# A transformer block on one NeuronCore: the first MLP sweep in steps of two tiles, output weights by quarter rows, two token tiles loaded by ScalarE's queue, and a new instruction order

## The chip, the cores and the metric

The kernel runs on one core of a Trainium2 chip. The core has five engines with a queue of instructions each: TensorE (PE in the profile; PEld is its loading of weights), VectorE (DVE), ScalarE (ACT), GpSimd (POOL) and SyncE (SP), which here only issues DMAs. ScalarE can issue DMAs as well. Each engine works its queue in order and waits on semaphores where it needs another engine's result. The metric is the device time of one execution in microseconds (us).

## The reference

The input is one sequence `x` of 2048 tokens and 512 channels, in bfloat16. A conditioning vector `c` gives six rows of 512 numbers by which two sub-blocks are shifted, scaled and gated.

```python
sa, ca, ga, sb, cb, gb = split((silu(c) @ w_mod), 6)
h = layernorm(x) * (1 + ca) + sa
x = x + ga * A(h)                       # attention
h = layernorm(x) * (1 + cb) + sb
out = x + gb * B(h)                     # MLP that mixes tokens
# A: 32 heads of 16 channels; a token sees itself and 7 others, 2, 4, ... 14 tokens back
q, k, v = split(h @ wqkv)
attn = softmax(q . k[t - 2w] / 4, w = 0..7);  A = (sum_w attn * v[t - 2w]) @ wo
# B: layernorm again, then over the TOKEN axis
u = gelu(layernorm(h).T @ w1 + b1)      # 2048 -> 1792
B = (u @ w2 + b2).T                     # 1792 -> 2048
```

## The kernel before

The 2048 tokens are 16 tiles of 128. They go through the attention half in five chunks of 2, 4, 4, 4 and 2 tiles (`SIZES`). For each chunk: LayerNorm statistics of a tile on VectorE or ScalarE (`ln1s`, `ln1v`, then `rstd1_`, `nb1_` for a group) and the normalized tile (`n1_`, on any of three engines); a transpose (`tr` on TensorE and its evictions `hT` in chunks 0 and 1, by DMA, `xt`, later); the projections `qkv<chunk>_<q, k or v><part>` on TensorE and their evictions `ev`; the products q*k on VectorE (`qk<chunk>_<0..3>`, 2.28 us each in a chunk of four tiles), summed over the head's channels by TensorE (`red`); the softmax, a chain over four engines: `max` (VectorE), `sub` (TensorE), `exp` (ScalarE), `esum` (TensorE), `rcp` (ScalarE), `smB` (VectorE). The probabilities and the values are then spread over the partitions by DMAs (`a2_<chunk>_<0..3>` and `vd<chunk>_<0..3>`), multiplied on VectorE (`pv`, again 2.28 us each), summed by TensorE (`pvacc`), evicted (`oev`) and multiplied with the output weights (`wo`). `x1_`, `ln2..`, `n2_`, `aff` and `ln3..`, `h3_` make the two further normalizations. For chunk 0 and 1 the unscaled projection weights are used, and the scale `a1col` is applied by the evictions `hT`; the scaled weights (`wsc`) serve the later chunks. `a1col` comes from `c`: `ld_c`, a small matmul `cps`, `silu_exp` (ScalarE), `silu_dve` (VectorE), and `modcols1` on TensorE, which also needs `ld_wmod1`.

The MLP needs every token for every output, so its first matrix product is cut into sweeps. `MIX` has two groups of rows of `u`: tiles 0 to 6 run over token tiles 0-5, 6-10 and 11-15, tiles 7 to 13 over token tiles 0-9 and 10-15. A sweep's partial sum is parked (`park`, ScalarE, in the tile `gT`), added later (`padd`) and put through `gelu`. In the order text, `mlp1_<sweep>_<row tile>_<first token tile>` is one step of such a sweep; its matmuls read `h3` of its token tiles. A step is issued as a whole on TensorE; before, the first sweep's steps hold four token tiles:

```python
steps = list(range(s_lo, s_hi, 4)) if not last else sorted(
```

`mlp2_<tile>` is the second product, `fin` and `st_out` finish and store a tile.

Nothing is ordered by a scheduler at run time. Each piece of work is named, and the text `ORDER` lists all of them in the order in which they are issued; each engine's queue is this list with the other engines' entries left out. A letter behind the name chooses the engine (`:a` ScalarE, `:d` VectorE, `:p` GpSimd, `:s` SyncE), `:q` cuts a matmul into four that write 32 partitions each, `:n` leaves an added identity matmul out, and `fill:62` issues matmuls of the identity that nobody reads, 62 times 128 columns in pieces of 512 and the rest of 128. `_Graph.schedule` (line 86) turns the text into the list and assigns the buffers; `ln_stats` (379), `build_chunk` (609) and the loops from line 918 on define the pieces. All instructions are recorded in one helper, so that every row of the profile has line 142 and pieces are told by their tiles: `psS` and `psL` are PSUM, `xx` the tokens, `big` the products, `vD` and `a2sb` what the two kinds of DMA write, `wst` staged weights, `woq` the output weights, `junk` the output of statistics on ScalarE.

`woq` holds 128 partitions of 4 x 512. Its source rows are numbered 16 h + 4 q + l; partition 32 l + h, column block q. Before, four DMAs (`ld_wo0` to `ld_wo3`) each bring one `l`: 32 partitions, four rows of 1 KB in each.

Of the kernel before, what the change touches and what calls it, by code (L numbers as in the profile page):

```python
# [196 lines left out]
ln1s11:a ln1s10:d ln1v10 ld_x_3_12 wsc1_1:p qvb0 qvb_cp0:d ev0_00:a qkv1_13 ld_wrow1 ld_b2 ln1s13:d qkv1_03 ev0_02:a  # L197
ln1v11 qkv1_10:q ln1v13 n1_9:a ev1_03:a qk0_1 qk0_0 ld_b1 ev1_13:a ld_wo3 ld_wqkv2 ld_x_4_14 ev1_10:a qkv1_00 ev1_00:a
wsc0_2:p qvb1 qvb_cp1:a red0_0 red0_1 qkv0_22:q ld_wo2 ld_wmod2 ln1s12:a qkv0_20 qk0_2 qk0_3 qk1_0 red0_2 red0_3
ev0_22:a ev0_20:a wsc0_1:a mask ln1v12 rstd1_3 qkv1_01 max0 ld_wrow3 ev1_01:a ld_wrow0 qk1_3 ld_wrow2 qkv1_11 sub0  # L200
# [6 lines left out]
oev0_0:a oev0_2:a smB1 wsc2_0:a wo0:q st_row1 ev2_12:a qk2_2 ev2_13:a qk2_3 wsc2_2:a x1_0:a wo1 x1_1:a vd1_2 qkv3_03
qkv2_22 biascols_cp:a a2_1_0:a qkv2_23 rstd1_4 a2_1_3:s nb1_4 qkv2_20 qkv2_21:q a2_1_2:s a2_1_1:s vd1_0 ln2q1:a
ln2q0:a n1_14:a ln2m0 ev3_03:a rstd2_0 red2_1 pv1_3 red2_2 n1_15:a red2_3 ev2_20:a vd1_1 nb2_0 ev2_22:a qkv3_11
ev2_21:a pvacc1_3 qkv3_12:q max2 sub2 n2_0:a ld_row1 qkv3_01 ev2_23:a qkv3_00:q ev3_11:a ev3_12:a oev1_3:a pv1_0  # L210
halo_k3:a exp2 pvacc1_0 oev1_0:a qkv3_02:q halo_v2:a qkv3_10:q ev3_02:a esum2 ev3_00:a vd2_3 xt14 pv1_2 rcp2 pvacc1_2
oev1_2:a pv1_1 pvacc1_1 oev1_1:a ev3_10:a n2_1:p aff0 ev3_01:a ln3s0:a smB2 qk3_0 qkv3_13:q vd2_1 qk3_2 wo5:q x1_5:a
wo2:q wo4 x1_2:a ev3_13:a x1_4:a qk3_1 wo3 a2_2_2:s ld_w1_0_512 ln2q5:a ln2q4:a ln2m4 x1_3:a vd2_2 red3_0 ln3s1:a
qkv3_22 ln2q2:a ln2q3:a ln3v0 qkv3_20:q rstd2_4 a2_2_3:s qkv3_21 ev3_20:a qkv4_00 ev3_21:a a2_2_1:s qk3_3 ln2m2
rstd2_2 qkv4_02 ev4_02:a a2_2_0:s pv2_3 nb2_2 n2_2:p qkv3_23 red3_1 vd2_0 ev4_00:a ld_w1_0_0 nb2_4 n2_4:a ld_w2_1
ev3_23:a red3_2 halo_v3:p ev3_22:a halo_v4:a vd3_0 red3_3 qkv4_20:q qkv4_12 max3 sub3 pv2_1 exp3 vd3_1 pvacc2_3 esum3
# [5 lines left out]
oev3_1:a park0_0:a park0_1:a ln2q6:a red4_0 pv3_3 pvacc3_3 oev3_3:a ln2q8:a pv3_2 park0_2:a mlp1_0_6_0:q pvacc3_0
ld_w1_0_896 pvacc3_2 mlp1_0_6_4:q oev3_2:a qk4_1 red4_1 vd4_0 ln2m6 rstd2_6 mlp1_0_4_0:q qk4_3 nb2_6 mlp1_0_4_4:q
oev3_0:a qk4_2 n2_8:d wo12:q n2_6:a n2_9:a ld_w2_2 park0_3:a park0_4:a park0_5:a x1_12:a park0_6:a ln2q12:a
mlp1_0_7_0:q mlp1_0_8_0:q ld_w2_4 n2_7:d aff6 ln3s7:a red4_2 red4_3 wo11:q x1_11:a ld_w2_0 max4 ld_w1_0_1152
mlp1_0_9_0 ln3s6:d ln3s8:d ln3s9:d sub4 ln3v6 ln3v9 exp4 wo13:n ln3v7 mlp1_0_10_0 ld_w1_0_1408 ln3v8 rstd3_6 x1_13:d
vd4_1 vd4_2 wo10:n nb3_6 h3_6:p h3_7:a mlp1_0_12_0 ln2q13:a mlp1_0_12_4 esum4 rcp4 x1_10:d mlp1_0_9_4 ln2m12 smB4
h3_8:d h3_9:p rstd2_12 nb2_12 n2_13:d a2_4_2:a mlp1_0_7_4 mlp1_0_7_8 mlp1_0_8_4 a2_4_0:a ln2q11:a n2_12:d aff12
mlp1_0_8_8 ln2q10:a a2_4_3:s mlp1_0_10_4 mlp1_0_9_8 mlp1_0_10_8 ln2m10 rstd2_10 inj1_3:qn park0_7:a park0_8:a a2_4_1:s
park0_9:a park0_10:a pv4_1 nb2_10 n2_11:a mlp1_0_11_0 mlp1_0_11_4 mlp1_0_11_8 pv4_0 pvacc4_0 pvacc4_1 n2_10:a  # L230
mlp1_0_12_8:q pv4_3 pv4_2 pvacc4_2 aff10 ln3s11:d park0_11:a pvacc4_3 ld_w1_0_1664 mlp1_0_13_0:q inj1_6:n oev4_0:a
oev4_2:a wo14:q ln3s10:a ln3s13:d x1_14 ln2s14 ld_w1_1_0 mlp1_0_13_4 park0_12:a ln2v14 wo15 ln3s12:a ld_w2_3 rstd2_14
ln3v11 x1_15 mlp1_0_13_8 ln3v10 rstd3_10 ln3v13 park0_13:a nb2_14 inj1_1:qn inj1_2:qn ln3v12 rstd3_12 n2_14:p ln2s15
ln2v15 nb3_10 mlp1_1_2_6 inj1_0:qn mlp1_1_0_6 mlp1_1_1_6 inj1_5:n ld_w1_1_640 aff14 mlp1_1_5_6 rstd2_15 nb2_15 n2_15:p
ln3s14:d ln3v14 h3_10:a mlp1_1_2_10 mlp1_1_1_10 aff15 rstd3_14 nb3_12 h3_12:p mlp1_1_0_10 park1_0:+ nb3_14 ln3s15:d
ln3v15 mlp1_1_5_10 mlp1_1_3_6 inj1_4:qn park1_1:+ rstd3_15 nb3_15 h3_15:d mlp1_1_4_6 mlp1_1_6_6 mlp1_1_6_10
ld_w1_1_896 ld_w1_2_0 h3_13:p mlp1_1_3_10 h3_14:a mlp1_1_4_10 ld_w1_1_1408 park1_2:+ park1_3:+ park1_4:+ h3_11:p
mlp1_1_7_10 padd1_7 gelu7 mlp1_1_8_10 padd1_8 mlp1_1_9_10 padd1_9 gelu9 mlp1_1_10_10 ld_w1_2_640 park1_5:+ mlp1_2_2_11
mlp1_2_3_11 mlp1_2_3_14 park1_6:+ padd2_3 mlp1_2_0_11 gelu3 gelu8 mlp1_2_2_14 padd2_2 mlp1_2_0_14 padd2_0 gelu0
ld_w2_5 mlp1_2_4_11 mlp1_2_4_14 padd2_4 padd1_10 mlp1_2_1_11 mlp1_2_1_14 gelu4 padd2_1 mlp1_2_6_11 ld_w2_7 gelu2  # L240
mlp1_2_5_11 mlp1_2_5_14 gelu1 padd2_5 gelu5 mlp1_1_11_10 mlp1_1_13_10 padd1_11 padd2_6 gelu6 mlp1_1_12_10 padd1_12
padd1_13 ld_w2_15 gelu11 gelu10 gelu12 mlp2_0_0 mlp2_0_0b gelu13 mlp2_0_0c fin0_0 st_out0_0 mlp2_4_0 mlp2_8_0 fin4_0
st_out4_0 fin8_0 mlp2_1_0 fin1_0 st_out1_0 st_out8_0 mlp2_6_0 ld_w2_13 mlp2_5_0 mlp2_3_0 mlp2_2_0 fin2_0 fin3_0 fin5_0
mlp2_7_0 ld_w2_9 ld_w2_11 mlp2_9_0 mlp2_10_0 st_out2_0 st_out3_0 fin6_0 st_out6_0 fin10_0 gsc fpre st_out5_0
st_out10_0 mlp2_14_0 fin9_0 st_out9_0 fin7_0 st_out7_0 fin14_0 mlp2_11_0 fin11_0 st_out11_0 st_out14_0 mlp2_12_0
fin12_0 mlp2_13_0 st_out12_0 fin13_0 st_out13_0 mlp2_15_0 fin15_0 st_out15_0 mlp2_15_1 fin15_1 st_out15_1 mlp2_15_2
# [822 lines left out]
```

## Time and profile before

| | |
|---|---|
| median of three runs | 203.14 us (202.55 to 203.84) |
| the profiled execution's own time | 202.81 us |
| its span, first to last instruction | 200.9 us |
| granted TensorE clock | 1.00 |
| instructions | 4468 |
| moved by DMA | 35.94 MB, mean 179 GB/s |

The costliest groups (line, engine, operation, out<-in, shapes, count, then busy us, mean ns of one, and the idle time just before them with what ended most of it):

```profile
L142 PE MATMUL psS<-h,wst 128*128 128x512 bf16 (+1 forms) x308 | 51.1, 379 | 0.1
L142 DVE TENSOR_TENSOR big<-a2sb,vD 128x4096 bf16<-128x4096 bf16 (+1 forms) x20 | 36.5, 1856 | 2.0 <-DMA vD<-v_sb 1.3
L142 DVE TENSOR_TENSOR big<-q_sb,k_f 128x4096 bf16<-128x4096 bf16 (+1 forms) x20 | 36.5, 1857 | 0.2 <-ACT q_sb L142 0.2
L142 ACT ACTIVATE junk<-xx 128x512 bf16<-128x512 bf16 x26 | 16.4, 632 | 3.0 <-DMA xx<-in_A_x_dram 1.4
```

Matmuls are pipelined: a 512-column one is listed with 379 ns, but the next can start 216 ns after it. So a busy TensorE may still be waiting, and its work is better counted by starts. Idle time is listed before the instruction that ends it.

### The profile page before, as it was taken

To read this page: it belongs to the slowest core of one execution; us is meant where nothing else is said; L and a number is where in the kernel's file an instruction comes from. 1 tells how busy PE (TensorE), PEld (TensorE's weight loads), DVE (VectorE), ACT (ScalarE), POOL (GpSimd) and SP (SyncE) were. 2 spreads that over 40 slices of the span, in tenths; PEclk is the share of its full clock that TensorE was granted. 3 is DMA by queue.
4 is the path that set the end of the run, shared out by engine and by line. 5 is a ranking of instruction groups with operands and counts; after the bars stand their busy time and mean duration, and the time that the engine had idled before them with its cause. 6 is when DMAs were issued, how large, how long until landed. Compare 5 with 4: busy or idle time off the path is not lost.

```text
span 200.9 us, 4468 instructions
## 1 busy us (share of the span) xinstructions
PE 190.1 (95%) x1778; PEld 95.1 (47%) x1778; DVE 159.1 (79%) x240; ACT 128.2 (64%) x308; POOL 18.1 (9%) x45
## 2 busy tenths in 40 slices
...
GB/s 169 330 378 286 304 198 89 208 217 86 259 3 280 291 303 123 172 302 284 237 151 135 31 167 220 157 129 298 337 41 26 26 77 328 211 93 26 52 82 52
DMA packets 53936, 35.94 MB, mean 179 GB/s; under 512 B 24476, under 2 KB 50716, under 8 KB 53916
## 3 DMA queue, kind: packets, MB, share of 16 engines
...
q14 instruction: 6, 0.05, 0.1%
...
## 4 chain that ended last, share of the span: by engine, by line
PE 66%; ACT 19%; DVE 9%; issue 3%; DMA 1%; SPq 0%; ACTq 0%; DVEq 0%
PE psS L142 64%; ACT junk L142 6%; DVE big L142 5%; ACT v_sb L142 3%; PE psL L142 2%; ACT h L142 2%; DVE h L142 2%; ACT xx L142 1%; ACT o_sb L142 1%; ACT q_sb L142 1%; ACT k_f L142 1%; DMA xx<-in_A_x_dram 1%; ACT hT L142 1%; ACT lv L142 1%; DVE woq L142 1%
## 5 line engine op out<-in xcount | busy, mean ns | idle before, releaser
L142 PEld LDWEIGHTS <-wst 128*128 128x128 bf16 (+1 forms) x482 | 34.9, 101 | 34.8 <-issue 4.5
L142 PE MATMUL psS<-h,wst 128*128 128x512 bf16 (+1 forms) x308 | 51.1, 379 | 0.1
L142 DVE TENSOR_TENSOR big<-a2sb,vD 128x4096 bf16<-128x4096 bf16 (+1 forms) x20 | 36.5, 1856 | 2.0 <-DMA vD<-v_sb 1.3
L142 DVE TENSOR_TENSOR big<-q_sb,k_f 128x4096 bf16<-128x4096 bf16 (+1 forms) x20 | 36.5, 1857 | 0.2 <-ACT q_sb L142 0.2
L142 DVE SCALAR_TENSOR_TENSOR h<-psS,bcol,rows_bc 128x512 f32<-128x512 f32 (+2 forms) x17 | 12.1, 709 | 22.6 <-PE psS L142 22.4
L142 PE MATMUL psS<-hT,w_qkv 128*32 128x512 bf16 (+3 forms) x300 | 29.3, 347 | 0.0
L142 PEld LDWEIGHTS <-w_qkv 128*32 128x32 bf16 (+1 forms) x342 | 19.7, 109 | 16.6 <-issue 3.3
L142 PE MATMUL psS<-gT,big 128*128 128x512 bf16 x112 | 24.8, 379 | 0.0
L142 ACT ACTIVATE junk<-xx 128x512 bf16<-128x512 bf16 x26 | 16.4, 632 | 3.0 <-DMA xx<-in_A_x_dram 1.4
L142 PEld LDWEIGHTS <-big 128*128 128x128 bf16 x144 | 12.0, 97 | 13.2
L142 PE MATMUL psS<-woq,o_sb 128*32 128x512 bf16 (+1 forms) x148 | 16.6, 380 | 0.7 <-ACT o_sb L142 0.7
L142 ACT ACTIVATE gT<-psS,bcol 128x512 bf16<-128x512 f32 x14 | 9.0, 685 | 8.6 <-DVE psS L142 8.4
L142 ACT ACTIVATE h<-xx,nb,rs 128x512 bf16<-128x512 bf16 x16 | 12.7, 812 | 2.4 <-DVE nb L142 2.4
L142 DVE TENSOR_TENSOR psS<-psS,gT 128x512 f32<-128x512 f32 x14 | 9.3, 694 | 6.1 <-PE psS L142 6.1
L142 POOL TENSOR_SCALAR h<-xx,rs,nb 128x512 bf16<-128x512 bf16 x9 | 6.9, 766 | 75.2 <-DVE mv L142 33.1
L142 PE MATMUL psS<-hT,wst 128*128 128x256 bf16 (+2 forms) x88 | 11.7, 343 | 0.8 <-ACT hT L142 0.8
L142 PEld LDWEIGHTS <-group 128*32 128x32 bf16 x288 | 6.5, 95 | 11.0 <-DVE big L142 4.0
L142 DVE TENSOR_TENSOR h<-h,xx 128x512 bf16<-128x512 f32 (+2 forms) x17 | 11.1, 652 | 0.7
L142 PE MATMUL psS<-big,group 128*32 128x512 bf16 (+1 forms) x160 | 9.6, 339 | 2.1 <-DVE big L142 2.0
L142 DVE TENSOR_TENSOR h<-h,rows_bc 128x1024 bf16<-128x1024 bf16 (+2 forms) x16 | 11.0, 690 | 0.4
L142 ACT ACTIVATE q_sb<-psS,qvb 128x512 bf16<-128x512 f32 (+1 forms) x20 | 11.2, 609 | 0.0
L142 ACT ACTIVATE v_sb<-psS,qvb 128x512 bf16<-128x512 f32 (+1 forms) x20 | 10.9, 603 | 0.0
...
## 6 DMA issues: line engine op xcount, KB each, us to landing
...
```

What stands on the lines that cost most here:

```text
L142: r = fn(*a, **k)
```

## The change

Four edits and a new list:

- The steps of the first sweep start at token tiles 0, 2, 4, 6 and 10 instead of every fourth tile from the sweep's first. The steps of the middle sweep (6, 10) stay.
- The output weights are brought by `q`: each of the four DMAs now writes all 128 partitions, one row of 1 KB in each.
- The loads of the first chunk's tiles and of chunk 1's two pairs may be issued by ScalarE. In the list one of them is: `ld_x_1_2`, ahead of `ld_c` and of the load of ScalarE's table.
- The choice of queues for `a2_` is written as a shared constant, which changes nothing.
- `ORDER` is another list. Some 40 pieces change their engine, 25 matmul steps become quartered and 21 whole ones, and there are eight fills (4, 64, 4, 13, 1, 1, 18, 14) instead of two (62, 17).

```diff
-ident act_table halo0 ld_x0 ln1s0:d ln1v0 ld_x1 ld_x_1_4 ld_c cps ln1s1:a ln1v1 rstd1_0 ln1s4:d consts nb1_0 ld_x_1_2
-ld_wmod1 fill:62 ln1s5:a ln1v4 ln1s3:d ln1s2:d ld_x_2_8 ld_wqkv1 ln1v3 silu_exp n1_0:a n1_1:p ld_x_2_6 ln1v2 ln1v5
-rstd1_1 ld_wqkv0 silu_dve modcols1 nb1_1 n1_3:a n1_4:d tr0_0 n1_2:d n1_5:d a1col wsc1_3:p hT0_2:a tr1_0 ln1s9:d
-wsc1_0:p hT0_3:a ln1s8:d ln1v8 ln1s6:d ln1v6 ln1s7:d tr1_2 hT0_1:a hT0_0:a hT1_0:a ln1v9 qkv0_10 ld_wmod0 qkv0_12
-qkv0_00 hT1_2:a ln1v7 hT1_3:d rstd1_2 nb1_2 ev0_10:a wsc1_2:p ev0_12:d n1_7:a modcols0 sab:a qkv0_02 hT1_1:d ld_x_3_10
+ident ld_x_1_2:a halo0 ld_c consts ld_x1:s ld_x0:s ld_x_1_4:s act_table ln1s3:d fill:4 cps ld_wmod1 silu_exp silu_dve
+fill:64 ln1s1:a ln1s2:a ln1s0:d ln1v1 ld_x_2_8 ln1v0 ln1s4:d ld_wqkv0 rstd1_0 nb1_0 n1_1:a fill:4 ln1v4 n1_0:p ln1s5:d
+ln1v2 ln1v5 ln1v3 rstd1_1 nb1_1 ld_x_2_6 modcols1 n1_2:d n1_5:d ln1s8:a a1col wsc0_3:p n1_4:d tr0_0 hT0_1:a hT0_3:a
+n1_3:d hT0_0:a fill:13 hT0_2:a ld_wqkv1 ld_wmod0 ln1s9:d ld_x_3_10 ln1s6:d tr1_0 tr1_2 hT1_2:a ln1v6 qkv0_02 ln1v9
+hT1_0:a qkv0_12 qkv0_10 ln1s7:d ln1v7 ln1v8 rstd1_2 hT1_3:d wsc1_0:a ev0_12:a modcols0 sab:a ld_x_3_12 nb1_2 n1_8:a
+qkv0_00 qvb0 wsc0_0:p ev0_10:a ld_b2 ld_wo1 hT1_1:d qkv1_00 ln1s11:d ln1s10:d ln1s13:d qkv1_10:q ln1v11 ln1v10
...
-ev1_11:a qk1_1 exp0 ln1s15:a qkv1_22 n1_8:p qkv1_02 wsc0_3:p ev1_02:a ld_wo1 modrow0 n1_6:p xt6 esum0:q rcp0 smB0
-qkv1_12:q ev1_12:a vd0_0 modrow1 ln1s14:a qkv1_21:q xt8 a2_0_1:a qk1_2 qkv1_23:q vd0_2 a2_0_3:s nb1_3 n1_13:p wsc2_3:a
-red1_0 a2_0_2:s red1_1 ev1_21:a mrows0:a red1_2 a2_0_0:s red1_3 n1_11:p ln1v14 qkv1_20:q n1_10:a mrows1 n1_12:a ln1v15
-wsc0_0:a qkv2_10:q ev2_10:a ev1_22:a max1 sub1:q exp1 vd0_1 qkv2_03:q pv0_0 pvacc0_0 qkv2_00 ev1_23:a ev1_20:a qkv2_01
-ev2_00:a ev2_03:a qkv2_11 pv0_2 st_row0 esum1:q halo_v1:p qkv2_02 ld_wo0 pv0_1 pvacc0_1 ev2_11:a vd0_3 rcp1 pvacc0_2
+wsc0_2:p ld_wo0 n1_7:p sub0 rstd1_3 qkv1_01 ld_wo2 exp0 qkv1_12:q wsc1_1:p esum0:q qk1_3 red1_0 ev1_01:a qk1_1
+ev1_02:a biascols n1_6:p ld_wrow1 rcp0 smB0 ev1_12:a ld_x_4_14 ln1s14:a qkv1_22 qk1_2 a2_0_2:a xt6 ld_wrow3 modrow1
+red1_1 a2_0_1:a n1_9:p wsc2_0:d ln1s15:a ln1v14 nb1_3 n1_11:a qkv1_23:q mrows1 qkv1_21 ev1_21:a red1_2 red1_3 xt8
+ev1_23:a fill:1 n1_10:p qkv1_20 ev1_20:a ev1_22:a qkv2_13 qkv2_10 wsc0_1:p vd0_2 ev2_13:a ln1v15 vd0_1 max1 sub1
+qkv2_00 exp1 a2_0_0:s a2_0_3:s pv0_1 vd0_0 pv0_0 st_row0 pv0_2 qkv2_03 esum1:q ld_wo3 pvacc0_0 vd0_3 halo_v2:p
...
-ln3s4:a wo7 nb3_0 ln3s2:d vd4_3 ln3v3 a2_3_0:s h3_1:a ln3v2 rstd3_2 vd3_2 ln3s5:a pv3_1 nb3_2 h3_3:d h3_0:p h3_2:d
-x1_7:a x1_8:a wo6:q x1_6:a wo9 pvacc3_1 ln3v4 ln3v5 rstd3_4 x1_9:a pv3_0 mlp1_0_3_0 mlp1_0_5_0 mlp1_0_1_0 mlp1_0_0_0
+oev2_1:a wo6 wo9 wo7 aff4 nb3_0 ln3s2:d ev4_02:a ln3s3:a ln3v3 h3_1:p wo8 a2_3_2:s ev4_00:a ln3v2 ld_w2_0 ln3s4:d
+rstd3_2 nb3_2 x1_9:a ln3s5:a h3_0:p mlp1_0_6_0:q x1_7:a ln3v4 x1_8:a h3_3:d mlp1_0_1_0 h3_2:d mlp1_0_6_2 mlp1_0_1_2
+pv3_1 mlp1_0_5_0:q ln3v5 ev4_10:a ld_w1_0_896 x1_6:a mlp1_0_3_0:q mlp1_0_3_2:q ln2q7:a pvacc3_1 rstd3_4 mlp1_0_5_2:q
...
-    wo_view = A_wo.rearrange("(h q l) n -> l h q n", h=H, q=4, l=4)
+    wo_view = A_wo.rearrange("(h q l) n -> q l h n", h=H, q=4, l=4)
...
+    QS = (("sp", nc.sync), ("act", nc.scalar))
...
+    def dma2(out_ap, in_ap, nbytes, writes, name):
+        return G.add_any([(n_, 0.5, lambda q_=q_: q_.dma_start(out_ap, in_ap)) for n_, q_ in QS], writes=writes, name=name,
+                         bytes_=nbytes / 350e3, lat=2.0, desc=1 + nbytes // 16384)
...
     for st in range(SIZES[0]):
-        dma(xx[:, st, :], x_view[:, st, :], P * D * 2, [], [("xx", st)], f"ld_x{st}")
+        dma2(xx[:, st, :], x_view[:, st, :], P * D * 2, [("xx", st)], f"ld_x{st}")
...
-            dma(xx[:, t:t + 2, :], x_view[:, t:t + 2, :], 2 * P * D * 2, [], [("xx", t), ("xx", t + 1)], f"ld_x_{ch}_{t}")
+            (dma2 if ch == 1 else lambda o, i, n, w, m: dma(o, i, n, [], w, m))(
+                xx[:, t:t + 2, :], x_view[:, t:t + 2, :], 2 * P * D * 2, [("xx", t), ("xx", t + 1)], f"ld_x_{ch}_{t}")
...
     for l in range(4):
-        dma(woq[32 * l:32 * l + 32, :, :], wo_view[l], 32 * 4 * D * 2, [], [("woq", l)], f"ld_wo{l}", rate=110e3)
+        dma(woq[:, l, :], wo_view[l], 32 * 4 * D * 2, [], [("woq", l)], f"ld_wo{l}", rate=110e3)
...
-                for n_, q_ in (("sp", nc.sync), ("act", nc.scalar))],
+                for n_, q_ in QS],
...
-                steps = list(range(s_lo, s_hi, 4)) if not last else sorted(
+                steps = [t for t in (0, 2, 4, 6, 10) if s_lo <= t < s_hi] if not last else sorted(
                     set([s_lo] + [t for t in T0[:-1] if s_lo < t < s_hi]))
```

More of the change, by code (lines that the diff above doesn't have):

```diff
@@ L197 @@
[L197 to L200, printed above, removed]
-ev1_11:a qk1_1 exp0 ln1s15:a qkv1_22 n1_8:p qkv1_02 wsc0_3:p ev1_02:a ld_wo1 modrow0 n1_6:p xt6 esum0:q rcp0 smB0
@@ L207 @@
[L207 to L216, printed above, removed]
@@ L222 @@
[L222 to L231, printed above, removed]
@@ L232 @@
[L232 to L246, printed above, removed]
@@ new lines @@
+qkv0_00 qvb0 wsc0_0:p ev0_10:a ld_b2 ld_wo1 hT1_1:d qkv1_00 ln1s11:d ln1s10:d ln1s13:d qkv1_10:q ln1v11 ln1v10
+qvb_cp0:a ev0_00:a ln1s12:a ev0_02:d qkv1_13 ld_wqkv2 qkv0_20 ln1v13 qk0_3 qk0_2 ev1_13:a qk0_0 qvb1 ln1v12 qkv0_22:q
+ld_wrow0 red0_0 ev1_00:a qkv1_03:q ev1_10:a qk0_1 red0_1 red0_2 red0_3 mask qvb_cp1:a ev0_20:a ev0_22:a wsc1_2:p
+halo_v1:a qk1_0 ev1_03:a wsc1_3:a qkv1_11:q ld_wmod2 wsc2_3:a modrow0 ld_b1 mrows0:a ev1_11:a ld_wrow2 qkv1_02 max0
+wsc0_2:p ld_wo0 n1_7:p sub0 rstd1_3 qkv1_01 ld_wo2 exp0 qkv1_12:q wsc1_1:p esum0:q qk1_3 red1_0 ev1_01:a qk1_1
```

45 lines of the change are left out of this document (40 added, 5 removed).

## The prediction

> **What bounds the kernel now.** I read the busy shares first, then busy time by stretches whose borders I took from the trace, then the starts on each engine in the first 18 us, then the gaps of VectorE.
>
> ```profile
> PE 190.1 (95%) x1778; PEld 95.1 (47%) x1778; DVE 159.1 (79%) x240; ACT 128.2 (64%) x308; POOL 18.1 (9%) x45
> ```
>
> TensorE looks full, but its ends are modelled. The stretches say more (length, then busy us of PE, PEld, DVE, ACT, POOL, clock, DMA share, GB/s):
>
> ```profile
> 2.50:8.43 5.93, 5.93 (x18) 2.29 (x19) 3.89 (x15) 4.43 (x14) 1.43 (x9) 1.00 0.94 297
> 8.43:11.44 3.01, 2.19 (x43) 1.86 (x41) 2.82 (x9) 2.43 (x6) 0.79 (x2) 1.00 1.08 374
> 11.44:17.26 5.82, 5.82 (x71) 5.20 (x71) 5.07 (x16) 5.25 (x14) 4.75 (x7) 1.00 1.10 345
> 17.26:131.48 114.22, 110.26 (x1319) 54.49 (x1318) 110.37 (x146) 103.86 (x260) 9.43 (x14) 1.00 0.72 192
> 131.48:200.90 69.42, 65.93 (x334) 31.28 (x331) 36.92 (x58) 10.97 (x16) 0.07 (x1) 1.00 0.44 129
> ```
>
> From 17.26 (the first q*k product) to 131.48 (`nb3_15`, the last normalization's bias) VectorE works 110.37 of 114.22 us. TensorE's starts, at 0.216 us a 512-column matmul of 128x128, leave several us open there: from 77 to 90.2 alone it waits or fills for 4.7. After 131.48 the rest is the MLP, 65.9 us of matmuls without a gap, and 3.5 us of tail; its first step, `mlp1_1_7_10`, starts at 132.21 and reads `h3_14` and `h3_15`, done at 132.15 and 132.09. So the time is: start of VectorE's long run, its work, its few waits, and 69.4 us that the change leaves alone. The start, on TensorE (start, length, what, and in brackets the idle time before):
>
> ```profile
> 2.50 0.18 PE L142 MATMUL psS<-ident,c_t 4*128 4x4 bf16 x1 [2.50 <-DMA c_t<-in_c_dram]
> 2.61 5.98 PE L142 MATMUL psS<-ident 128*128 128x512 bf16 x17
> 8.43 0.54 PE L142 MATMUL psS<-sc,big 128*128 128x1 bf16 x16
> 8.84 1.78 PE L142 MATMUL psS<-ident,h 128*128 128x128 bf16 x24
> 11.44 2.78 PE L142 MATMUL psS<-hT,wst 128*128 128x256 bf16 x24 [0.83 <-ACT hT L142]
> ```
>
> and the only long waits of VectorE's run:
>
> ```profile
> 38.84 1.23 DVE L142 TENSOR_TENSOR big<-a2sb,vD 128x2048 bf16<-128x2048 bf16 x1 [1.31 <-DMA vD<-v_sb]
> 115.34 1.22 DVE L142 TENSOR_TENSOR big<-a2sb,vD 128x2048 bf16<-128x2048 bf16 x1 [0.48 <-issue]
> ```
>
> **The start.** ScalarE's queue now issues the pair `ld_x_1_2` (256 KB), then `ld_c`, then loads its table. An issue there takes 0.57 us (`c_t`), so `ld_c` is issued at 0.85 + 0.57 = 1.42, and the table ends at 0.85 + 1.14 + 1.28 = 3.3. Where `c_t` lands is not shown. One end: 1.65 us after its issue, as now (0.85 to 2.50), 3.07. The other: behind the pair, as loads on SP's queue land in order; `ld_x0` (128 KB) is there at 3.01, and 384 KB more at 297 GB/s end at 4.3. I take 4.3, since SP's rows are many. The Trainium skill (DMA: Bandwidth & Descriptors, Queues, rings and completion order) has each queue's descriptors consumed in ring order on each DMA engine, and engines alternating between queues; by it the later landing holds, and no run here shows it for ScalarE's queue.
>
> Behind `cps` now stand `fill:64` and `fill:4`, 17 matmuls of 512 columns in place of 15 and two short ones. The 62 of now took 5.8 us because about the first twelve started 0.427 us apart, and only from 7.5 us on, 5.0 us after the first, they came at 0.216. (The clock column reads 1.00 there; the pace is read from the starts.) With the same 5.0 us: 4.45 + 5.0 + 5 x 0.216 = 10.6 for `modcols1`, against 8.43. If all 17 are slow: 11.7. With `c_t` at 3.07: 9.35. The Trainium skill (TensorE: Matmul & The Clock Gate, What's actually happening) names 3.4 us of sustained work in a free-running window; by that `modcols1` could start at 9.8, and the sum below would be 0.6 less; the trace's own 5.0 us is longer.
>
> `a1col` and `tr0_0` follow: 0.54 and 0.56 of matmuls and the hand-over to ScalarE, 1.15; then the four evictions `hT0_*` (now 9.82 to 11.39, 1.57), and 0.05 to the first projection: 10.6 + 1.15 + 1.57 + 0.05 = 13.35 against 11.44, +1.9. `fill:13` (0.9 us) lies under the evictions. The other path is earlier: ScalarE has `silu_exp` (4.5), behind it `ln1s1` and `ln1s2` (1.26 each, to 7.15), `rstd1_0`, `n1_1`, `rstd1_1`, `ln1s8`, free for `hT0_1` at 11.1. VectorE waits in `silu_dve` before `ln1s0`; its LayerNorm work is behind that. From the first projection to the first product there are four projections, `modcols0` and `qvb0` in both orders (5.82 us), in the new one with an eviction less; so the run starts 1.8 later, at 19.1 (ends +0.55 and +2.9).
>
> **VectorE's work.** From the first product to `nb3_15` the same 40 products stand in both orders. By their rows, there come to it `wsc2_0` (0.4), `ln3s4` (0.69), `n2_14`, `h3_7` and `h3_9` (0.41 each); there go `ln3s13` (0.68), `n2_8`, `n2_13` (0.41 each), and `park1_1` (0.66), now behind `nb3_15`: 2.3 - 2.2, +0.2 with the roundings. Ahead of the first product `ln1s5`, `ln1s11`, `n1_3`, `ev0_02` come and `ln1s2`, `ln1s8`, `ev0_12`, `qvb_cp0` go: 11.6 becomes 11.8, under the longer start. ScalarE loses 4.9 us of its work ahead of `nb3_0` (86.34), but it is idle 10 us of the stretch, so that buys nothing while VectorE is full. If ScalarE were the gate there, it would be worth up to what TensorE waits, 5.
>
> **Waits of VectorE.** `pv0_3` waits 1.31 for `vd0_3`, issued 4.5 us after `smB0` behind three `a2` issues, `vd0_1`, `st_row0`, `ld_wo0`. In the new order two of the `a2` are ScalarE's (0.6 to 0.7 of it each, covered by its idle 10), and `vd0_3` is sixth, at about 3.5 us; `pv0_3` is wanted 0.4 later (`wsc2_0`). 1.4 against 1.31, but the same two heavy followers (`ld_row0`, `xt10`) share its engines: -1.0 (ends -1.31 and 0). `pv4_*` has 0.6 us more work ahead of it than its 0.48 wait: -0.4. New waits cannot be read off this trace: 0 to +2.2 (what all waits over 0.15 us of the run sum to now). I take +0.3, near the lower end, because nearly all of the run's 146 instructions now find their operands ready.
>
> **Edits with one answer.** Two-tile steps issue the same matmuls; the sweep can start on `h3_0`, `h3_1`. That is worth nothing while `h3_15` sets the end: TensorE has 40.7 us of work from there to `mlp1_1_7_10` in 42. Quarter rows: 128 packets of 1 KB as before, landing in 6.3 to 6.8 us; `woq_s` reads them at 42.18, the last was issued at 33.36, cover 2 us, in the new order about 1.9; gone, it would stop VectorE by the lack. Four more changes between whole and quartered matmuls (0.1 us each) and 1.7 us of fills lie in TensorE's waits. The output stage stands in another order, but each tile has 3.02 us of matmul over 1.44 of VectorE, and `ld_w2_15` is issued some 9 us before its use, with 5.7 us to land: 0.
>
> **Sum.** +1.8 + 0.2 - 1.4 + 0.3 = +0.9. The profiled execution took 202.81 us (span 200.9 and 1.9 around it), 0.33 below the median of 203.14; so 203.7 for such a one, and **204.0** as a median.
>
> **Rivals.** *Faster.* `c_t` is not held up (+0.55), both landings vanish (-1.8), and ScalarE's 4.9 us free VectorE's small gaps (3.85 in all, of which 1.8 counted): -1.5 to -2.5, 200.6 to 201.6. For it: the chain of waits runs through ScalarE from 62 to 91. Against: VectorE has no gap over 0.11 from 62 to 90. 12%, the part under 201.1. *Slower.* The start costs it all: `c_t` behind the pair and 17 slow fills, `modcols1` at 11.7 or later, +2.9; the waits of VectorE are exchanged for others. It decides when `modcols1` starts after about 11. 203.14 + 2.9 + 0.2 + 0 to 1.5 = 206.2 to 207.7. For it: the fills wait on nothing and stand ahead of `modcols1` by order. 28%, with the upper part of the forecast's case. *It does not do what it says:* a pair on ScalarE's queue brings data no sooner, as 297 GB/s flow from 2.5 us on anyway; I have counted it at nothing.
>
> **Numbers.** My case, between 201.1 and 205.2: 60%. About 1%, 2 us, can be told from no change. Low end: +0.55 + 0.2 - 1.8 - 0.8 of small gaps, 201.3. High end: +2.9 + 0.2 + 0.8, 207.0. Faster 0.12, same 0.60, slower 0.28.
>
> **What would show it.** `modcols1` at 10.6 and the first projection at 13.3; `c_t`'s first reader at 4.3; VectorE's first product at 19.1 and a run of 113 us from there; no 1.3 us wait before `pv0_3`; 65.9 us of matmuls after `mlp1_1_7_10`. I am wrong if the start is early, if VectorE has gaps of over 2 us in its run, or if its run ends before TensorE asks for it.

## The result and the profile after

The changed kernel takes 201.42 us (median of 21 runs, 201.01 to 202.16); the kernel before, run beside it, 202.72 us (21 runs). The ratio is 0.994, with a 95% interval of 0.9921 to 0.9958: faster by about 0.6%, 1.3 us. The forecast was 204.0 us, 0.9 slower. In two more groups of runs, on other chips, its ratio was 0.991 (intervals below).

The profiled execution of the changed kernel took 202.11 us, span 200.4, so it is one of its longest runs. Below are two more profiles of the same kernel, with spans of 199.6 and 199.9. First the stretches, cut as before (length, then busy us of PE, PEld, DVE, ACT, POOL, clock, DMA share, GB/s), the run from VectorE's first product to `nb3_15`, and the rest:

```profile
18.80:130.90 112.10, 109.62 (x1360) 54.79 (x1364) 110.08 (x146) 103.46 (x256) 8.99 (x13) 1.00 0.67 187
130.90:200.40 69.50, 66.11 (x330) 31.47 (x334) 37.67 (x59) 11.10 (x16) 0.81 (x2) 1.00 0.47 135
```

The run starts 1.54 us later than before (17.26), and it is 2.12 us shorter (114.22). What follows it is the same, 69.5. VectorE is busy for all but 2.02 us of the run, where it was idle for 3.85. All its waits over 0.15 us in that stretch, and one just ahead of it (`q_sb`), in the view of waits (who waits for what, us, times, longest):

```profile
DVE big L142 <- ACT q_sb L142: 0.4, 1, 0.4
DVE xx L142 <- PE psS L142: 0.2, 1, 0.2
DVE q_sb L142 <- ACT qvb L142: 0.2, 1, 0.2
DVE gT L142 <- PE psS L142: 0.2, 1, 0.2
```

The last one (`park1_1`) stands behind `nb3_15`. Neither of the two long waits of before is there: the four `pv0_` products stand in one row, starting at 36.22, with no idle time ahead of any:

```profile
36.22 4.65 DVE L142 TENSOR_TENSOR big<-a2sb,vD 128x2048 bf16<-128x2048 bf16 x4
```

The start on TensorE (start, length, what, idle time before):

```profile
1.43 0.61 PE L142 MATMUL psS<-ident 128*128 128x512 bf16 x1 [1.43 <-POOL epscol L142]
3.98 0.18 PE L142 MATMUL psS<-ident,c_t 4*128 4x4 bf16 x1 [1.94 <-DMA c_t<-in_c_dram]
4.10 6.58 PE L142 MATMUL psS<-ident 128*128 128x512 bf16 x17
10.52 0.54 PE L142 MATMUL psS<-sc,big 128*128 128x1 bf16 x16
```

`c_t` is read at 3.98, `modcols1` starts at 10.52 (forecast 10.6), the first projection at 13.19 (forecast 13.3), the first product at 18.80 (forecast 19.1). So in this execution the start went as forecast, in part by luck: the first fill behind `cps` started 0.35 us earlier than forecast (4.10, not 4.45), and the pace changed 5.5 us after it, not 5.0. It is not the usual start, as the next section shows.

### The profile page after: what moved, and what is told of

It is laid out like the page before. It is cut to its first block, busy times and chain, and to the rows that moved or that the text cites. A ratio compares the mean times of both kernels' runs of the same rounds, so it can differ in the third digit from the quotient of the medians.

```text
span 200.4 us, 4572 instructions
## 1 busy us (share of the span) xinstructions
PE 191.0 (95%) x1818; PEld 95.8 (48%) x1836; DVE 159.6 (80%) x241; ACT 128.6 (64%) x306; POOL 18.6 (9%) x45
## 4 chain that ended last, share of the span: by engine, by line
PE 69%; DVE 22%; issue 4%; DMA 1%; ACT 1%; ACTq 0%; DVEq 0%
PE psS L142 67%; DVE big L142 14%; PE psL L142 3%; DVE st L142 2%; DVE h L142 2%; DMA c_t<-in_c_dram 1%; DVE mv L142 1%; ACT h L142 1%; DVE lsb L142 1%; DVE m L142 1%; DVE nb L142 0%; ACTq L142 0%; DVE woq L142 0%; DVE hT L142 0%; ACT rb L142 0%
## 5 line engine op out<-in xcount | busy, mean ns | idle before, releaser
L142 PE MATMUL psS<-h,wst 128*128 128x512 bf16 (+1 forms) x333 | 50.3, 380 | 0.5 <-issue 0.3
L142 PE MATMUL psS<-woq,o_sb 128*32 128x512 bf16 (+1 forms) x107 | 15.7, 380 | 0.9 <-ACT o_sb L142 0.6
L142 PEld LDWEIGHTS <-ident 128*32 128x32 bf16 (+1 forms) x137 | 7.0, 102 | 10.5 <-issue 5.9
L142 PE MATMUL psS<-ident 128*128 128x512 bf16 (+1 forms) x35 | 10.6, 450 | 1.4 <-POOL epscol L142 1.4
L142 PE MATMUL psS<-hT,wst 128*32 128x512 bf16 (+2 forms) x110 | 11.7, 352 | 0.1
L142 DVE BATCH_NORM_STATS2 st<-xx 128x6 f32<-128x512 bf16 x12 | 7.9, 680 | 3.9 <-DMA xx<-in_A_x_dram 3.8
```

The source lines that it names most:

```text
L142: r = fn(*a, **k)
```

## The experiments

Each group of runs stood on one chip, with the kernel before beside it; a ratio is to that kernel and has its 95% interval. Since the starts of one kernel differ between executions by about 1 us, I also read from each trace the length of VectorE's run, from the start of its first product to the start of `nb3_15`: in the kernel before it was 114.22, in three profiles of the changed kernel 112.09 to 112.10.

Theory 1 was the prediction's: the time is the start of VectorE's run, plus its work and waits, plus 69.5. Theory 2 was that ScalarE's chain, which the profile of before shows from 62 to 91 us, set the time, and that its 4.9 us less work made the gain.

### The start

**control**: the changed kernel again.

> The changed kernel once more, unaltered, to have it beside the edits on one chip and a second profile. All theories: ratio 0.994 to the kernel before (0.992 to 0.996). The theory that the start's slow fills end at a moment that differs from execution to execution expects that, in this profile, the time at which the fills go from 0.427 to 0.216 us apart is not the 9.75 us of the first profile, and that the span has moved by about half as much in the same direction; the rival, that the spread of 201.0 to 202.2 us comes from transfers, expects the same moment or a span that does not follow it.

201.31 us, ratio 0.9907 (0.9888 to 0.9927), a little below the expected range. The pace changed at 6.97 us, not 9.62, and everything from the first projections on stands 0.75 us earlier, to the end. On TensorE and VectorE:

```profile
4.10 5.19 PE L142 MATMUL psS<-ident 128*128 128x512 bf16 x17
9.13 0.54 PE L142 MATMUL psS<-sc,big 128*128 128x1 bf16 x16
```

```profile
3.78 0.69 DVE L142 BATCH_NORM_STATS2 st<-xx 128x6 f32<-128x512 bf16 x1 [3.78 <-DMA xx<-in_A_x_dram]
...
7.70 0.16 DVE L142 SCALAR_TENSOR_TENSOR nb<-mv,rs 128x2 f32<-128x2 f32 x1 [0.86 <-ACT rs L142]
...
9.50 0.16 DVE L142 SCALAR_TENSOR_TENSOR nb<-mv,rs 128x4 f32<-128x4 f32 x1 [0.60 <-ACT rs L142]
...
10.36 0.15 DVE L142 TENSOR_SCALAR a1col<-psS 128x4 f32<-128x4 f32 x1
```

The same 17 fills take 1.39 us less (their last is `fill:4`). But `a1col` starts without idle time ahead of it: `modcols1` is no longer what VectorE waits for, as it was in the first profile:

```profile
11.10 0.16 DVE L142 TENSOR_SCALAR a1col<-psS 128x4 f32<-128x4 f32 x1 [0.66 <-PE psS L142]
```

VectorE is now held by its own LayerNorm work, which waits 3.78 us for the pair of tiles, then twice for ScalarE. The first product is at 18.06, 0.80 later than before.

The moment of the change of pace in the profiles that have the changed kernel's start, with the first product:

| profile | fills at 0.216 us from | first product |
|---|---|---|
| control | 6.97 | 18.06 |
| a2_sp2 | 7.49 | 17.80 |
| rows_nofill | 8.18 | 18.30 |
| control_b | 8.76 | 18.34 |
| the first profile | 9.62 | 18.80 |
| a2_sp | 10.03 | 18.96 |
| merged4 | 10.15 | 19.09 |
| a_dly_a | 10.30 | 19.25 |

Up to about 8.8 the change of pace hardly matters (`a1col` waits for TensorE 0 us in the control and 0.15 in control_b; the landings of tiles move the start by a few tenths). Later, it delays the first product by a little over half as much (`a1col` waits 0.66 in the first profile, 0.86 in a_dly_a, where `c_t` was also read 0.26 later than in the control). That would fit the 201.0 to 202.2 us of the 21 runs, of which one has a profile.

**c_first**: `c_t` ahead of the pair.

```diff
-ident ld_x_1_2:a halo0 ld_c consts
+ident ld_c halo0 ld_x_1_2:a consts
```

> ld_c is put ahead of the pair ld_x_1_2 on ScalarE's queue, all else as in the changed kernel. Theory 1 (the time is the start of VectorE's run plus its work and waits plus 69.5): c_t's reader starts at 2.6 to 3.1 in place of 3.98, modcols1 at 9.0 to 9.6 in place of 10.5, VectorE's first product about 1.0 to 1.3 earlier than 18.8, and the ratio falls from 0.994 to about 0.988. Theory 2 (the gain comes from ScalarE's smaller load between 60 and 91 us, and a later start is taken up by slack before that): the first product is as much earlier, but the ratio stays at 0.993 to 0.995.

0.9922 (0.9892 to 0.9953). `c_t` was read at 2.21 and `modcols1` started at 8.04. Yet the first product came at 18.37, since the list has VectorE begin with `ln1s3`, which reads the pair, and that now landed later:

```profile
5.30 0.69 DVE L142 BATCH_NORM_STATS2 st<-xx 128x6 f32<-128x512 bf16 x1 [5.30 <-DMA xx<-in_A_x_dram]
```

Both theories had expected a first product 1.0 to 1.3 us earlier than 18.80; it came 0.43 earlier, and 0.31 later than in the control. So an earlier `modcols1` brought nothing, and the run does not tell the two theories apart.

**early_fill**: six of the fills ahead of `cps`.

```diff
-ln1s3:d fill:4 cps ... fill:64 ln1s1:a
+ln1s3:d fill:24 cps ... fill:44 ln1s1:a
```

> Six of the start's fills (24 in the list's units) are put ahead of cps, where TensorE is idle between 2.0 and 4.0 us, and eleven (44) stay behind it; the same number in all. Theory 1 with the reading that TensorE's slow pace ends about 5 us after it starts to work without a break: the fills run from 1.43 on, the pace changes at 5 to 8 us instead of 9.75, modcols1 starts at 7.5 to 8.5 instead of 10.5, VectorE's first product is 1 to 2 us earlier and the ratio falls to 0.985 to 0.990. Theory 2: modcols1 as early, ratio unchanged at 0.993 to 0.995. If the slow pace ends at a fixed time after the span's start, and not after TensorE's own, modcols1 moves by less than 0.5.

0.9948 (0.992 to 0.9975). The pace changed at 5.41, `modcols1` started at 8.31, now waiting 0.80 for its weights. First product 18.19: no gain on the control, where theory 1 had 1 to 2 us. VectorE waited as in the control, 3.75 + 1.04 + 0.60.

**fast_start**: VectorE begins with the tile that lands first.

```diff
-ld_x1:s ld_x0:s ld_x_1_4:s act_table ln1s3:d fill:4 cps ld_wmod1 silu_exp silu_dve
-fill:64 ln1s1:a ln1s2:a ln1s0:d ln1v1 ld_x_2_8 ln1v0 ln1s4:d ld_wqkv0 rstd1_0 nb1_0 n1_1:a fill:4 ln1v4 n1_0:p ln1s5:d
-ln1v2 ln1v5 ln1v3 rstd1_1 nb1_1
+ld_x0:s ld_x1:s ld_x_1_4:s act_table ln1s0:d ln1v0 ln1s3:d fill:24 cps ld_wmod1 silu_exp silu_dve
+fill:44 ln1s1:a ln1s4:d ln1v1 ld_x_2_8 rstd1_0 ln1s5:d ln1s2:a ld_wqkv0 nb1_0 ln1v4 n1_0:p n1_1:d
+ln1v5 ln1v3 ln1v2 rstd1_1 nb1_1
```

> The changed kernel with another start: ld_x0 first on SP's queue and ln1s0 (which reads it) first on VectorE, in place of ln1s3, which waits for the pair on ScalarE's queue; six fills ahead of cps; rstd1_0 ahead of ln1s2 on ScalarE, ln1s5 ahead of nb1_0 and n1_1 on VectorE. Theory 1, as the first runs have changed it (the start is set by VectorE's waits for the first tiles and for ScalarE, 3.78 + 0.86 + 0.60 us in the second profile, and by the fills only where the pace changes late): VectorE starts at 3.0, nb1_1 stands at 8.6 to 8.9 in place of 9.5, the first product is 0.6 to 0.9 earlier than 18.06, ratio 0.986 to 0.990 where the changed kernel has 0.991 to 0.994. Rival (the start is set by TensorE's way from modcols1 to the projections): first product at 17.9 or later, ratio unchanged.

0.9918 (0.9888 to 0.9948), first product 17.97: a miss. I had put `rstd1_0` ahead of `ln1s2` on ScalarE; it waited 0.78 there for `ln1v1`, `ln1s2` ended at 8.56, and `rstd1_1` behind it at 9.38, about as late as in the control (9.47).

**fast_start2**: the same, with ScalarE's order mended.

```diff
-fill:44 ln1s1:a ln1s4:d ln1v1 ld_x_2_8 rstd1_0 ln1s5:d ln1s2:a ld_wqkv0 nb1_0 ln1v4 n1_0:p n1_1:d
-ln1v5 ln1v3 ln1v2 rstd1_1 nb1_1
+fill:44 ln1s1:a ln1s2:a ln1s4:d ln1v1 ld_x_2_8 rstd1_0 ln1s5:d ld_wqkv0 ln1v4 ln1v5 ln1v3 ln1v2 nb1_0 n1_0:p n1_1:d
+rstd1_1 nb1_1
```

> The changed kernel with the start of fast_start, but ln1s2 ahead of rstd1_0 on ScalarE, and rstd1_1 directly behind that. Theory 1 (VectorE's start hangs on ScalarE's chain ln1s1, ln1s2, rstd1_0, n1_1, rstd1_1): without n1_1 in it rstd1_1 ends at 8.2 to 8.4 in place of 9.4, nb1_1 stands at 8.3 to 8.6 in place of 9.5, the first product at 17.0 to 17.5, ratio 0.985 to 0.989. Rival (something behind it, such as the evictions hT0 or the loads of the weights, sets the first projection): nb1_1 as early, the first product at 17.8 or later, ratio 0.990 to 0.993.

200.93 us, 0.9893 (0.9872 to 0.9915). `nb1_1` stood at 8.35, `a1col` at 9.38, the first product at 16.80, 1.26 earlier than in the control, and the last instruction as much earlier. So the floor of the start was LayerNorm on VectorE and ScalarE, with the order of the first tiles; how much of it is the load order and how much ScalarE's order was not tried apart.

**b_pair**: the kernel before, with the pair on ScalarE's queue ahead of `ld_c`, and nothing else.

```diff
-ident act_table halo0 ... ld_x_1_4 ld_c cps ... consts nb1_0 ld_x_1_2
+ident ld_x_1_2 ld_c act_table halo0 ... ld_x_1_4 cps ... consts nb1_0
...
+            if (ch, t) == (1, 2):
+                add("act", 0.55, lambda: nc.scalar.dma_start(xx[:, 2:4, :], x_view[:, 2:4, :]), writes=[("xx", 2), ("xx", 3)],
+                    name="ld_x_1_2", lat=2.0)
+                continue
```

> The kernel before with one edit: ld_x_1_2 is issued by ScalarE, ahead of ld_c, and no longer by SP. The prediction's reckoning: c_t is read at 3.9 to 4.3 in place of 2.5, and the fills with it, so that modcols1 starts at 9.3 to 11 and VectorE's first product 0.5 to 1.9 later, ratio 1.003 to 1.010. Theory 1 as changed (the fills count only where the pace changes late, else VectorE's and ScalarE's LayerNorm): c_t as late, first product 0 to 1.0 later, with ln1s2 and ln1s3, which read the pair, up to 1 us earlier.

1.0036 (1.0008 to 1.0063). `c_t` was read at 3.61 and the first product came at 18.22, 0.96 later. Both paths were later by as much: `modcols1` at 9.30, and ScalarE's first tile, which waited for `x1` until 4.28 in place of 3.46. In the list of before, the pair alone costs.

### VectorE's waits, and who else is the gate

**b_vd3**: the kernel before, with one issue moved on SP's queue.

```diff
-vd0_1 qkv2_03:q pv0_0 pvacc0_0 qkv2_00 ... st_row0 ... ld_wo0 pv0_1 pvacc0_1 ev2_11:a vd0_3 rcp1
+vd0_1 qkv2_03:q pv0_0 pvacc0_0 vd0_3 qkv2_00 ... st_row0 ... ld_wo0 pv0_1 pvacc0_1 ev2_11:a rcp1
```

> The kernel before, with one edit: vd0_3 is issued ahead of st_row0 and ld_wo0 on SP's queue, 1.3 us sooner. Theory 1: the wait of 1.31 us before pv0_3 falls to 0 to 0.3, the rest moves up with it, ratio 0.994 to 0.996. Theory 2: the wait goes, but what is won is waited out before 91 us, ratio 0.998 to 1.000. If st_row0 and ld_wo0, later by one issue, become late for woq_s, the gain is given back there.

201.85 us, 0.9928 (0.9901 to 0.9955). The wait before `pv0_3` is gone and VectorE's run measures 112.90, 1.33 less. `woq_s` did not wait. The four products stand in one row (of b_vd3_b, the same kernel):

```profile
34.85 4.62 DVE L142 TENSOR_TENSOR big<-a2sb,vD 128x2048 bf16<-128x2048 bf16 x4
```

**a2_sp**: the two `a2_0_` transfers of ScalarE's queue given back to SP, at their places in the list.

```diff
-a2_0_2:a xt6 ... a2_0_1:a n1_9:p
+a2_0_2:s xt6 ... a2_0_1:s n1_9:p
```

> The two a2_0 transfers that the changed kernel gives to ScalarE's queue (jj 2 and 1) go back to SP's, ahead of the two that are there. Theory 1: SP issues vd0_3 some 1.2 us later (two issues of 0.6), pv0_3 waits for it again, 0.6 to 1.2 us, and the ratio rises from 0.994 to 0.997 to 1.000. Theory 2: at most a short wait there, made good before 91 us, ratio 0.993 to 0.996.

209.79 us, 1.0331 (1.0306 to 1.0356). The edit did more than I meant. On SP's queue, `a2_0_2` waits for `smB0`, and `xt6`, `ld_wrow3`, `xt8`, `vd0_2`, `vd0_1` stand behind it; TensorE then waits for `ld_wrow3` (SP's issues, then TensorE):

```profile
31.74 0.74 SPq L142 DMA_DIRECT2D a2sb<-lsb  x1
32.60 1.35 SPq L142 DMA_TRANSPOSE hT<-h  x1
34.01 0.56 SPq L142 DMA_DIRECT2D gT<-in_w_mod_dram  x1
```

```profile
37.47 1.15 PE L142 MATMUL psS<-gT,sc 128*32 128x128 bf16 x36 [6.07 <-DMA gT<-in_w_mod_dram]
```

It tells nothing on the question it was made for, but shows that an issue that waits holds up the others queued behind it. The 8.5 us against the control are not that wait alone: the granted clock was 0.71 in it and 0.64 in the 4.5 us behind it.

**a2_sp2**: the same two, put directly ahead of the `a2_0_0` and `a2_0_3` that SP already has.

```diff
-a2_0_2:a xt6 ... a2_0_1:a n1_9:p ... a2_0_0:s a2_0_3:s pv0_1
+xt6 ... n1_9:p ... a2_0_2:s a2_0_1:s a2_0_0:s a2_0_3:s pv0_1
```

> The changed kernel with the two a2_0 transfers of ScalarE's queue put on SP's directly ahead of the two that are there, so that nothing else is held up behind smB0: vd0_0, st_row0, ld_wo3 and vd0_3 are issued 1.2 to 1.3 us later. Theory 1: pv0_3 waits again, 0.5 to 1.3 us, VectorE's run from qk0_3 to nb3_15 is that much longer than 112.1, ratio 0.994 to 0.999. Rival (the wait went because vd0_3's packets meet less traffic, not because of its place): no wait over 0.3, run 112.1 to 112.4.

0.9954 (0.993 to 0.9978); run 113.05, 0.95 longer:

```profile
39.59 1.23 DVE L142 TENSOR_TENSOR big<-a2sb,vD 128x2048 bf16<-128x2048 bf16 x1 [0.91 <-DMA vD<-v_sb]
```

The place in the queue, not lighter traffic, took that wait away.

**b_dly_d, b_dly_a, b_dly_p**: the kernel before, with needless work on one engine behind `red3_0`. VectorE's is shown; ScalarE's is two activations of the same size, TensorE's is `fill:24` in the list.

```diff
-vd2_2 red3_0 ln3s1:a
+vd2_2 red3_0 dly ln3s1:a
...
+    def f_dly():
+        for _ in range(2):
+            nc.vector.tensor_tensor(jkd[:], ident[:].unsqueeze(1).to_broadcast([P, 4, P]), ident[:].unsqueeze(1).to_broadcast([P, 4, P]), op=ALU.add)
+    add("dve", 1.3, f_dly, reads=["ident"], writes=["jkd"], name="dly")
```

> The kernel before, with two additions of 128x512 on VectorE that nobody needs, behind red3_0 in the list (67 us). What they take is read from their row. Theory 1 (VectorE is the gate from its first product to nb3_15): the time grows by about that row, ratio 1.000 plus row over 202.8. Theory 2 (ScalarE's chain is the gate from 62 to 91): VectorE is not, so by less than a third of it.

> The kernel before, with two activations of 128x512 on ScalarE that nobody needs (about 1.3 us), behind red3_0. Theory 1: 0 to +0.3 us, ratio 1.000 to 1.0015. Theory 2: +1.0 to +1.3 us, ratio 1.005 to 1.0065.

> The kernel before, with six matmuls of 512 columns on TensorE that nobody needs (6 x 0.216 = 1.3 us), behind red3_0. Theories 1 and 2: 0 to +0.3 us, ratio 1.000 to 1.0015, as TensorE waits 2 us in each 10 there. A third theory, that TensorE has been the gate of the stretch all along: +1.3 us, 1.0065.

Ratios 1.0045 (1.0014 to 1.0077), 1.0111 (1.0067 to 1.0154) and 1.0061 (1.0024 to 1.0097). VectorE's two additions took 0.84 us; 0.78 of that stood at `pv2_3`, and 0.43 was left of the run's length, as later and earlier waits shrank. ScalarE's 1.25 us lengthened the run by 1.24, which is 0.6%; its ratio is larger, and its profile is of the shortest of its six runs (204.13 us, median 205.19), so what the others add is not seen. Of TensorE's 1.3 us, 0.86 arrived (the run was 1.84 longer, but 0.98 stood there before the added work: its wait before `pv0_3` was 1.74). VectorE now waits for ScalarE and for TensorE, in the second and third of these kernels:

```profile
73.35 0.16 DVE L142 TENSOR_TENSOR mv<-mv,sums 128x2 f32<-128x2 f32 x1 [0.73 <-ACT junk L142]
```

```profile
76.97 1.22 DVE L142 TENSOR_REDUCE m<-psL 128x128 bf16<-128x1024 f32 x1 [0.77 <-PE psL L142]
```

So neither theory holds for the kernel before: near 70 us its order leaves none of the three engines much room. ScalarE's idle 10 us lie mostly elsewhere in the 114 us. From 65 to 75 it works 9.81 of 10 us in the kernel before (the fourth busy figure; columns as in the first block above):

```profile
65.00:70.00 5.00, 5.00 (x40) 1.89 (x39) 4.90 (x5) 4.94 (x17) 0.00 (x0) 1.00 0.91 269
70.00:75.00 5.00, 5.00 (x64) 3.44 (x66) 4.82 (x6) 4.87 (x15) 0.00 (x0) 1.00 0.97 311
```

TensorE, estimated from its starts at 0.216 us for 512 columns, has about 0.7 of these 10 us open; 2 in 10 is about its mean from 60 to 90.

**a_dly_a**: the same delay of ScalarE in the changed kernel.

```diff
-a2_2_3:s red3_0 wo3:q
+a2_2_3:s red3_0 dly wo3:q
```

> The changed kernel with the same two needless activations (1.25 us) on ScalarE behind red3_0 that made the kernel before 1.24 us longer in VectorE's run. If the change has given ScalarE slack there (4.9 us less work ahead of nb3_0): the run grows by 0 to 0.4 us, and ScalarE was a second gate before and is none now. If it has not: +0.9 to +1.3 us.

0.9947 (0.9922 to 0.9972); run 112.45, so of 1.25 us only 0.35 arrived. The wait is at the same instruction, shorter:

```profile
75.85 0.16 DVE L142 TENSOR_TENSOR mv<-mv,sums 128x2 f32<-128x2 f32 x1 [0.31 <-ACT junk L142]
```

The change did give ScalarE room, some 0.9 us at this place.

### The edits counted at nothing

**rows_nofill** (whole rows of the output weights, no fills of 1, 1, 18 and 14) and **merged4** (the steps of tiles 0, 1 and 2, 3 side by side, shown for one of the fourteen blocks).

```diff
-    wo_view = A_wo.rearrange("(h q l) n -> q l h n", h=H, q=4, l=4)
+    wo_view = A_wo.rearrange("(h q l) n -> l h q n", h=H, q=4, l=4)
-        dma(woq[:, l, :], wo_view[l], 32 * 4 * D * 2
+        dma(woq[32 * l:32 * l + 32, :, :], wo_view[l], 32 * 4 * D * 2
```

```diff
-mlp1_0_5_0:q ln3v5 ev4_10:a ... rstd3_4 mlp1_0_5_2:q
+ln3v5 ev4_10:a ... rstd3_4 mlp1_0_5_0:q mlp1_0_5_2:q
```

> The changed kernel with the output weights by whole rows as before, and without the four fills of the middle (1, 1, 18, 14). Theory 1: VectorE's run from qk0_3 to nb3_15 stays at 112.1 us within 0.3, ratio 0.991 to 0.994. Rival (quarter rows bring woq_s its operands in time, or the fills keep TensorE's pace up): woq_s waits, or the matmuls after 82 us are slower, and the run grows by 0.5 to 2 us.

> The changed kernel with the step of tiles 0 and 1 of the first sweep put directly ahead of the step of tiles 2 and 3, for each of the fourteen blocks, so that both start when the four tiles are there, as one step of four did. Theory 1: TensorE has slack there, run of 112.1 to 112.4 us, ratio 0.991 to 0.995. Rival (the two-tile steps fill TensorE's holes, and what is late there is late for VectorE's red, sub and projections): run longer by 0.5 to 1.5 us.

0.9918 (0.9887 to 0.9949) and 0.9936 (0.9913 to 0.996). In the first, VectorE takes 99.73 us from `smB0` to `nb3_15`, in the control 99.76 (its run from the first product, 111.78, is shorter: a wait of 0.91 for a tile stands ahead of that product, and the wait of 0.36 for `q_sb` behind it is gone). In the second the run is 112.33: 0.23 more, as `x1_14` waits 0.48 for TensorE instead of 0.25. Quarter rows and middle fills, tried only together, are worth nothing here; two-tile steps, 0.2 us in one profile.

### Three kernels on one chip

**control_b**, **fast_start2_b** and **b_vd3_b** are the changed kernel, fast_start2 and b_vd3 again.

> The changed kernel beside the two that follow, on one chip: ratio 0.990 to 0.995, VectorE's run from qk0_3 to nb3_15 112.1 us, first product at 18.0 to 19.3, by the moment at which the fills change their pace.

> The changed kernel with the shorter start of fast_start2, unaltered, beside the changed kernel. If the start's 1.26 us (first product at 16.80 against 18.06) reach the end: 1.0 to 1.6 us less than the changed kernel, ratio 0.984 to 0.989. If most of it is lost in the usual execution (late change of pace, late tiles): within 0.5 us of it.

> The kernel before with vd0_3 ahead of st_row0 and ld_wo0, unaltered, beside the changed kernel. If one moved issue is worth as much as the whole change: ratio within 0.003 of the changed kernel's. If the change brings more: 0.003 to 0.007 above it.

| kernel | median us | ratio | first product | run |
|---|---|---|---|---|
| before | 203.69 | | 17.26 (its one profile, other chip) | 114.22 |
| b_vd3: one issue moved | 201.94 | 0.9928 (0.9904 to 0.9952) | 18.06 | 112.84 |
| the changed kernel | 201.67 | 0.9913 (0.9888 to 0.9937) | 18.34 | 112.10 |
| fast_start2 | 200.64 | 0.9864 (0.9839 to 0.9889) | 17.22 | 112.09 |

One moved issue brings about as much as the whole change; the two ratios cannot be told apart. fast_start2 has the run of the changed kernel and a start 1.1 us shorter, ends 1.0 us earlier, and beats both. Its VectorE, where the control waited 3.78, 0.86 and 0.60:

```profile
3.36 0.69 DVE L142 BATCH_NORM_STATS2 st<-xx 128x6 f32<-128x512 bf16 x1 [3.36 <-DMA xx<-in_A_x_dram]
...
5.72 0.69 DVE L142 BATCH_NORM_STATS2 st<-xx 128x6 f32<-128x512 bf16 x1 [0.32 <-DMA xx<-in_A_x_dram]
...
7.93 0.16 DVE L142 SCALAR_TENSOR_TENSOR nb<-mv,rs 128x2 f32<-128x2 f32 x1 [0.20 <-ACT rs L142]
...
8.45 0.16 DVE L142 SCALAR_TENSOR_TENSOR nb<-mv,rs 128x4 f32<-128x4 f32 x1
...
9.48 0.15 DVE L142 TENSOR_SCALAR a1col<-psS 128x4 f32<-128x4 f32 x1
```

## Why the prediction was wrong

The mechanism was right in its outline: a later start against shorter waits, and an end that stays. The sign came out wrong because two terms of the sum were mis-sized, each by about a microsecond: the start was usually some 1.0 shorter than forecast, and VectorE's run 1.2 shorter (its waits 0.7, its work 0.5). In the first pair of profiles:

| term | forecast | measured |
|---|---|---|
| start of VectorE's run | +1.8 | +1.54 (0.80 and 1.08 in two more profiles) |
| VectorE's work | +0.2 | -0.29 (busy time of the run) |
| its waits, old and new | -1.1 | -1.83 |
| what follows `nb3_15` | 0 | +0.08 |
| span | +0.9 | -0.5 (-1.2 and -0.9) |

From 204.0 to 201.4 are 2.6 us: 0.7 from the waits, 0.5 from the work, 1.0 from the start if the usual one is the control's, and 0.4 because the kernel before had a median of 202.72 over 21 runs, not 203.14 over three. The start's share is the least sure: the first product comes at 17.18 to 18.06 in six profiles with the start of before (mean 17.59) and at 17.80 to 19.25 in the eight of the table above (mean 18.58), so by the means the start costs 1.0, not 0.8. The measured time is just above the forecast's low end, 201.3, which had both long waits gone, as they were.

- **The start** failed in the step from `cps` to `modcols1`. The text took the pace to change 5.0 us after the first matmul, as in the one profile it had. In the profiles with either start it came 2.9 to 5.9 us after the fills began to run without a break. The rule it weighed there, 3.4 us of sustained work in a free-running window (the Trainium skill, TensorE: Matmul & The Clock Gate, What's actually happening), comes with a warning that the number of slow matmuls changes from run to run with the window's phase. The traces agree that the number changes: 7 slow fills behind `cps` in the control, 13 in the first profile. That a window's phase is the reason, no run here shows, and the measured 2.9 to 5.9 us reach well beyond the rule's 3.4. By 9.8 for `modcols1` the sum would have been 0.3, still not faster. The larger omission was the second path: with fills out of the way, LayerNorm on VectorE and ScalarE holds the start at about 18.1. I called that path earlier, from ScalarE's rows, and did not follow VectorE's own waits through it.
- **c_t behind the pair**, 4.3 forecast and 3.98 found, was right; c_first shows the other order, 2.21. What I drew from the Trainium skill on it (DMA: Bandwidth & Descriptors, Queues, rings and completion order), that a queue's descriptors are consumed in ring order, agrees with both. (In b_pair `c_t` was read at 3.61, 0.3 before the pair had landed whole.)
- **"The pair brings data no sooner"** was wrong as a statement: it landed at 3.80, in the kernel before at 5.36. It was right as a price: b_pair is slower, as `x1` and `c_t` pay.
- **The wait before `pv0_3`** was forecast to shrink by 1.0 and went wholly. The issue came 3.3 us behind `smB0` (forecast 3.5), and the margin was enough; a2_sp2, with the issue at 4.7, has 0.91 of it. So the two `a2_0_` issues on ScalarE's queue are the part of the list with a shown gain; the other 0.8 of the 2.1 us by which the run is shorter was not taken apart. The wait before `pv4_1` went too (-0.48 against -0.4). Two waits of 0.2 for ScalarE, which the sum left out, went as well, and new ones of 0.37 and 0.25 came, more than the +0.3 allowed. The rest, 0.26, is in gaps under 0.15.
- **VectorE's work** did grow by its rows, which add up to 119.42 in place of 119.18, but the busy time fell by 0.29, as more rows overlap their neighbours. An addition of rows does not see that. What made them overlap was not tried.
- **"ScalarE's idle 10 us, so its relief buys nothing"** rested on VectorE as the only gate, and on an idle share of the whole run where ScalarE is busy for 9.81 of 10 us near 70. b_dly_a shows it false for the kernel before: 1.24 of 1.25 us arrived. In the changed kernel ScalarE has room there (a_dly_a); whether that ended the two waits of 0.2 was not tried.
- **The rival "faster"** had the measured time in its range of 200.6 to 201.6; its 12% were for the part under 201.1. Of its conditions, both landings vanished, and of the small gaps 0.26 us went; `c_t` was held up all the same, which costs little where the pace changes early (early_fill: `modcols1` 0.8 earlier than in the control, no gain). **The rival "slower"**, decided by `modcols1` later than about 11, came near that in one profile (10.97), and there the first product was 1.99 late; the waits it thought exchanged were not.
- **Counted at nothing** and found so: quarter rows, middle fills, the output stage and its order (69.50 against 69.42). Two-tile steps: 0.2 at most.
